# Pacing the first forty transfers of a fused attention and MoE kernel by the fourth ahead

## The chip, the cores and the metric

The kernel runs on one core of a Trainium2 chip. The metric is the time of one execution in microseconds of device time; three runs were made of the kernel before. Engines are called as in the profile: PE is TensorE's matmul, PEld its weight load, DVE VectorE, ACT ScalarE, POOL GpSimd, SP SyncE. SP computes nothing here; it issues transfers (DMAs).

## The reference, cut to what matters

Chunked attention comes first: 4 batches of 8 heads, sequences of 768, head size 64. Each chunk of 32 queries looks at 16 keys to its left, its own 32, 8 to its right and 8 memory keys, 64 in all. The attention's output, as a matrix x of 3072 tokens by 512, then goes through a two-layer block with a rational function between the layers.

```python
for c in range(nc):
    k_full = np.concatenate([mem_k, k_ctx], axis=2)
    v_full = np.concatenate([mem_v, v_ctx], axis=2)
    scores = scale * np.matmul(q_c, k_full.transpose(0, 1, 3, 2))
    a = np.exp(scores - np.max(scores, axis=-1, keepdims=True))
    a = a / (np.sum(a, axis=-1, keepdims=True) + 1e-09)
    out[:, :, c_start:c_end] = np.matmul(a, v_full)
...
h = x @ w_in
P = a[0] + a[1] * h + a[2] * h2 + a[3] * h3
Q = 1.0 + np.abs(b[0]) * np.abs(h) + np.abs(b[1]) * h2
return ((P / (Q + 1e-06)) @ w_out).astype(np.float32)
```

The weights w_in (512 x 2048) and w_out (2048 x 512) are handed over as 64-bit floats, bit for bit.

## The kernel before, in words

**Tiling.** The 3072 tokens are six blocks of 512. The hidden size 2048 is sixteen slices of 128. A step n stands for one (block, slice): g1 (L480) makes h, 128 x 512, in 12 matmuls (L489); the chain of lines L557 to L614 computes the rational function on ACT, DVE and POOL; g2 (L491) adds its product with w_out into four accumulators in another 12 matmuls (L504). Each weight and each x is split into a high and a low part, hence three matmuls for every product.

**Attention.** A unit is (block i, pair of heads p). For the first two blocks its pieces are: the load of queries and keys (q), of values (v); scores on PE (b, L361), maximum, difference and exponential on DVE and ACT (L369, L379, L396), zeroing of absent keys on POOL (L392), transposes on PE (c, L412), a copy (L419), the product with the values (d, L428) and the sums (L434), the division (L444), transposes back (L454), and the split into x_hi and x_lo.

**Weights.** Each weight tile arrives as raw 64-bit words (w, w_load) and is converted by five tokens: A (ACT, L183), B (DVE, L187), C (DVE, L192), H (ACT, L199), L (POOL, L204).

**Order.** The first part of the program is a list of tokens written out by hand (SEQ); function hand turns each into instructions, which every engine keeps in program order. All transfers go through one helper, load (L145), and nearly all of them through SP's queue, in program order. The transfers are counted in this document from 1 in the order in which load is called:

- 1: w_in slice 0. 2 and 3: queries and keys of unit (0,0), one transfer for each head. 4 and 5: (0,2). 6 and 7: (0,1). 8 and 9: values of (0,0). 10 and 11: queries and keys of (0,3). 12: w_out slice 0. 13: the six parameters, a few bytes.
- 14 and 15: values of (0,2). 16 and 17: values of (0,1). 18: w_in slice 1. 19 and 20: queries and keys of (1,0). 21 and 22: values of (0,3). 23 and 24: w_in slices 3 and 2.
- 25 to 28: queries and keys of (1,1) and (1,2). 29 and 30: values of (1,0). 31: w_in slice 4. 32: w_out slice 1. 33 and 34: values of (1,1). 35: w_in slice 5. 36 and 37: values of (1,2). 38: w_out slice 2. 39 and 40: queries and keys of (1,3).

Queries and keys are 64 rows of 4,608 bytes (294,912 bytes), values 64 rows of 4,096 (262,144), a weight half 128 rows of 4,096 (524,288).

The framework tells the landing of a transfer by a semaphore and uses eight of them in turn, so that SP holds a transfer back until the eighth ahead of it has landed. A transfer also waits until its buffer is clear: for the memset of its pads or for the last reader of the buffer's former content.

Of the kernel before, what the change touches and what calls it, by code (L numbers as in the profile page):

```python
# [37 lines left out]
XL_POOL = [(0, 0), (0, 2), (1, 0), (1, 1), (1, 2)]  # L38
WARM = 14
CLEAR = [("qk", 0, "vp"), ("qk", 3, "ap"), ("qk", 1, "pv"), ("qk", 2, "vv"), ("v", 1, "pa"), ("v", 2, "pv"), ("v", 0, "pp"), ("v", 3, "pp")]  # L40
LEAD = 22
WHEN = dict(b=0, m=1, x=2, c=2, z=3)
WAIT = 4
# [46 lines left out]
def attn_moe(ctx, tc, qk, vm, w, ab, out, seq):  # L90
# [50 lines left out]
    def pin(ins):  # L141
        if pinned[0]:
            tc.keep_in_program_order(ins)

    def load(dst, src, queue=nc.sync):  # L145
        ins = queue.dma_start(out=dst, in_=src)
        if in_order[0]:
            tc.keep_in_program_order(ins)

# [12 lines left out]
    def w_load(kind, j):  # L162
        if kind == "in":
            raws[j] = slot(RAW_SLOTS[j], "w_raw", U32)
        if j < WHOLE:
            load(half(raws[j], kind), half(w_bits_of[j][:, :4 * DM], kind))
        elif kind == "in":
            load(raws[j], w_bits_of[j][:, :4 * DM])
# [55 lines left out]
    def load_qk(i, p, t, queue=nc.sync):  # L224
        u = unit.setdefault((i, p), {})
        u["q"], u["k"] = [], []
        for h in range(2):
            load(rows(t[:, h * NK:h * NK + NK + NQ], h), qk[i, p, h], queue)
        for c in range(NC):
            u["q"].append(t[:, NK + c * CHUNK:NK + (c + 1) * CHUNK])  # L230
            first = t[:, start_in(c):start_in(c) + KEYS]
            u["k"].append(bass.AP(first.tensor, first.offset, [list(first.ap[0]), [NK + NQ, 2], [1, KEYS]]))
# [392 lines left out]
    def plan(n, kind, i, p):  # L625
        att.setdefault((n, kind), []).append((i, p))

    units = [(i, p, base) for i in range(3, NBLK)
             for p, base in enumerate(BASES.get(i, [first[i] - LEAD + 4 * p for p in range(NPAIR)]))]
    went = []  # L630
# [34 lines left out]
    def begin():  # L665
        pick = {"a": nc.scalar, "v": nc.vector, "p": nc.gpsimd}
        for name, n, who in CLEAR:
            engines = [pick[x] for x in who]
# [175 lines left out]
```

## Time and profile before

| what | value |
|---|---|
| median of 3 runs | 599.34 us (598.25 to 599.51) |
| the profiled execution's own time | 598.73 us |
| its span, first to last instruction | 596.9 us |
| around the span | 1.8 us |
| granted TensorE clock, mean of the span | 1.000 |
| PE busy | 586.8 us, 98% |
| DVE, ACT, POOL busy | 464.9, 401.9, 406.4 us |

The span is what the profile explains; the 1.8 us around it are the start and the end of the program. The profiled execution was 0.61 us shorter than the median. A PE that is busy for 98% of the span leaves about 10 us in which it had nothing to do. Slices in the page are a fortieth of the span, 14.9 us.

### The profile page before, as it was taken

To read this page: it belongs to the slowest core of one execution; us is meant where nothing else is said; L and a number is where in the kernel's file an instruction comes from. 1 tells how busy PE (TensorE), PEld (TensorE's weight loads), DVE (VectorE), ACT (ScalarE), POOL (GpSimd) and SP (SyncE) were. 2 spreads that over 40 slices of the span, in tenths; PEclk is the share of its full clock that TensorE was granted. 3 is DMA by queue.
4 is the path that set the end of the run, shared out by engine and by line. 5 is a ranking of instruction groups with operands and counts; after the bars stand their busy time and mean duration, and the time that the engine had idled before them with its cause. 6 is when DMAs were issued, how large, how long until landed. Compare 5 with 4: busy or idle time off the path is not lost.

```text
span 596.9 us, 13088 instructions
## 1 busy us (share of the span) xinstructions
PE 586.8 (98%) x5111; PEld 478.4 (80%) x5111; DVE 464.9 (78%) x762; ACT 401.9 (67%) x665; POOL 406.4 (68%) x376
## 2 busy tenths in 40 slices
PE   7899999999999999999999999999999999999997
PEld 6677888888787878878888888888888888888886
DVE  5899999898797759888877778787787766666673
ACT  4699999898667655656566666565765656755673
POOL 5468998798546766576677576766667677667682
PEclk9999999999999999999999999999999999999999
DMA  8965346230345344332331422312510100100001
GB/s 304 406 206 213 146 177 212 72 128 13 124 131 165 98 151 127 94 111 72 99 87 50 154 43 87 94 36 81 178 36 1 37 10 9 71 1 1 0 1 70
DMA packets 34591, 61.14 MB, mean 102 GB/s; under 512 B 4066, under 2 KB 20706, under 8 KB 34146
## 3 DMA queue, kind: packets, MB, share of 16 engines
q1 hardware_dynamic: 34386, 60.18, 30.6%
q8 instruction: 40, 0.66, 0.5%
q14 instruction: 21, 0.17, 0.1%
q10 hardware_dynamic: 144, 0.13, 0.1%
HBM read 44.56 MB, written 7.34 MB: 87 GB/s over the span
## 4 chain that ended last, share of the span: by engine, by line
PE 95%; DVE 2%; ACT 1%; DMA 1%; issue 0%; SPq 0%; POOL 0%; DVEq 0%
PE h L489 44%; PE o L504 43%; PE pairs L315 2%; PE pairs L293 2%; PE pa L428 1%; PE pa L361 1%; DMA qk<-in_qk_dram 1%; PE pa L412 1%; PE pa L454 0%; DVE e L379 0%; PE pa L434 0%; ACT e L396 0%; DVE ct L602 0%; ACT eT L419 0%; PE warm L663 0%
## 5 line engine op out<-in xcount | busy, mean ns | idle before, releaser
L489 PE MATMUL h<-x_hi,w_hl 128*128 128x512 f32 x768 | 240.3, 394 | 0.4 <-DVE ct L602 0.3
L504 PE MATMUL o<-w_hl,ghi 128*128 128x512 f32 x768 | 236.8, 390 | 0.0
L566 POOL TENSOR_TENSOR cy<-cy,ha 128x512 f32<-128x512 f32 x96 | 124.6, 1298 | 140.4 <-ACT cy L562 135.8
L504 PEld LDWEIGHTS o<-w_hl,ghi 128*128 128x128 f32 x768 | 143.9, 188 | 29.8 <-ACT v_main L546 0.2
L489 PEld LDWEIGHTS h<-x_hi,w_hl 128*128 128x128 f32 x768 | 141.7, 188 | 32.4 <-DVE ct L602 1.1
L489 PE MATMUL h<-x_lo,w_hl 128*128 128x512 f32 x384 | 150.0, 391 | 0.2 <-POOL x_lo L467 0.2
L504 PE MATMUL o<-w_hl,glo 128*128 128x512 f32 x384 | 150.0, 391 | 0.0
L614 POOL TENSOR_TENSOR glo<-ct,ghi 128x512 fp32r<-128x512 f32 x95 | 122.9, 1294 | 9.1 <-ACT ghi L609 3.2
L594 DVE SCALAR_TENSOR_TENSOR ct<-ct,par,h 128x512 f32<-128x512 f32 x82 | 61.2, 746 | 56.2 <-ACT h L590 55.5
L575 DVE TENSOR_TENSOR ct<-ct,h 128x512 f32<-128x512 f32 x96 | 65.6, 684 | 39.4 <-ACT ct L571 37.8
L586 ACT ACTIVATE h<-cy 128x512 f32<-128x512 f32 x82 | 49.1, 599 | 69.5 <-DVE ct L579 56.1
L557 ACT ACTIVATE ha<-h 128x512 f32<-128x512 f32 x96 | 57.4, 598 | 54.4 <-PE h L489 54.3
L607 POOL TENSOR_TENSOR ghi<-ct,zero 128x512 fp32r<-128x512 f32 x81 | 84.2, 1040 | 2.5 <-PE o L504 1.2
L504 PEld LDWEIGHTS o<-w_hl,glo 128*128 128x128 f32 x384 | 72.1, 188 | 16.8 <-POOL glo L614 1.6
L489 PEld LDWEIGHTS h<-x_lo,w_hl 128*128 128x128 f32 x384 | 72.1, 188 | 16.1 <-POOL x_lo L467 0.6
L562 ACT ACTIVATE cy<-ha,bab 128x512 f32<-128x512 f32 x96 | 78.4, 817 | 2.6
L571 ACT ACTIVATE ct<-h,par 128x512 f32<-128x512 f32 x96 | 73.6, 766 | 5.6 <-PE h L489 5.5
L579 DVE SCALAR_TENSOR_TENSOR ct<-ct,par,h 128x512 f32<-128x512 f32 x96 | 71.6, 746 | 3.0
L602 DVE SCALAR_TENSOR_TENSOR ct<-h,ct 128x512 f32<-128x512 f32 x82 | 56.5, 689 | 2.6
L598 DVE SCALAR_TENSOR_TENSOR h<-cy,h 128x512 f32<-128x512 f32 x82 | 56.5, 689 | 0.0
L590 ACT ACTIVATE h<-h 128x512 f32<-128x512 f32 x82 | 47.7, 582 | 2.6
L204 POOL TENSOR_TENSOR w_hl<-w_raw,w_hl 128x512 fp32r<-128x512 f32 x32 | 42.0, 1318 | 6.4 <-ACT w_hl L199 5.7
(80 smaller groups left out, 461.9 us busy)
## 6 DMA issues: line engine op xcount, KB each, us to landing
w_raw<-in_w_dram SPq DMA_DIRECT2D x26, 512.0 KB, 5.9
qk_pairs<-in_qk_dram SPq DMA_DIRECT2D x16, 576.0 KB, 4.2
v_main<-in_vm_dram SPq DMA_DIRECT2D x16, 512.0 KB, 5.1
out_dram<-v_main SPq DMA_DIRECT2D x23, 256.0 KB, 2.3
qk<-in_qk_dram SPq DMA_DIRECT2D x16, 288.0 KB, 5.8
eT<-blocks SPq DMA_DIRECT2D x64, 64.0 KB, 2.1
xf<-blocks SPq DMA_DIRECT2D x64, 64.0 KB, 2.1
v_main<-in_vm_dram SPq DMA_DIRECT2D x12, 256.0 KB, 6.4
```

The source lines that it names most:

```text
L489: pin(nc.tensor.matmul(h, lhsT=wt[:, cols], rhs=xt[i][:, ct, :], start=ct == m == 0, stop=ct == NCT - 1 and m == 2))
L504: ins = nc.tensor.matmul(o, lhsT=gt[:, cols], rhs=wt, start=begin and m == 0, stop=end and m == 2)
L557: pin(nc.scalar.activation(c["ha"], c["h"], AF.Abs))
L562: pin(nc.scalar.activation(c["y"], c["ha"], AF.Identity, scale=B1, bias=B0))
L566: pin(nc.gpsimd.tensor_tensor(c["y"], c["y"], c.pop("ha"), op=ALU.mult))
L571: pin(nc.scalar.activation(c["t"], c["h"], AF.Identity, scale=A3, bias=A2))
L575: pin(nc.vector.tensor_tensor(t, t, h, op=ALU.mult))
L579: pin(nc.vector.scalar_tensor_tensor(t, t, A1, h, op0=ALU.add, op1=ALU.mult))
L594: pin(nc.vector.scalar_tensor_tensor(t, t, A0, r, op0=ALU.add, op1=ALU.mult))
L598: pin(nc.vector.scalar_tensor_tensor(r, yy, QC, r, op0=ALU.add, op1=ALU.mult))
L607: pin(nc.gpsimd.tensor_tensor(ghi, chain[z]["t"], zero.broadcast_to([P, TB]), op=ALU.add))
L614: pin(engine.tensor_tensor(glo, chain.pop(z)["t"], gh[z].bitcast(F32), op=ALU.subtract))
```

## The change

A list of the transfers made so far is kept. Of the first forty, each from the fifth on gets a dependency on the one made four before it, of the kind that is kept with a semaphore: SP may issue it only when that transfer has landed. Sizes, order, queue, buffers and all other instructions are as before.

```diff
+AHEAD = 4
+PACED = 40
...
+    sent = []
+
     def load(dst, src, queue=nc.sync):
         ins = queue.dma_start(out=dst, in_=src)
+        sent.append(ins)
+        if AHEAD < len(sent) <= PACED:
+            tc.add_manual_dep(ins.ins, sent[-1 - AHEAD].ins.name, mybir.DependencyInfo(mybir.DependencyClass.Sync, mybir.DependencyReason.DATA), reason="pace")
         if in_order[0]:
             tc.keep_in_program_order(ins)
```

## Rows read from the trace of the kernel before

**Rows 1.** The page: the DMA's share and rate in 40 slices.

```profile
DMA  8965346230345344332331422312510100100001
GB/s 304 406 206 213 146 177 212 72 128 13 124 131 165 98 151 127 94 111 72 99 87 50 154 43 87 94 36 81 178 36 1 37 10 9 71 1 1 0 1 70
```

**Rows 2.** The page: the chain that ended last, shares of the span by engine.

```profile
PE 95%; DVE 2%; ACT 1%; DMA 1%; issue 0%; SPq 0%; POOL 0%; DVEq 0%
```

**Rows 3.** The chain that ended last in order of time, first 60 us: start, us, what.

```profile
2.19 4.35 DMA qk<-in_qk_dram
...
6.68 1.97 PE pa L361 x32
...
16.34 1.13 issue
17.47 0.60 PE pa L412 x4
...
28.30 2.69 PE h L489 x10
...
49.25 2.91 PE h L489 x12
```

**Rows 4.** Busy time of each engine in four stretches; the last three columns are PEclk, DMA share, GB/s.

```profile
5.00:13.00 8.00, 5.66 (x104) 4.87 (x104) 3.35 (x6) 1.79 (x3) 3.71 (x6) 1.00 0.98 355
13.00:30.00 17.00, 15.42 (x306) 11.98 (x305) 14.63 (x30) 11.13 (x22) 6.88 (x10) 1.00 1.03 404
39.00:43.00 4.00, 3.76 (x83) 3.00 (x85) 4.00 (x8) 3.47 (x7) 2.73 (x5) 1.00 0.89 274
80.00:83.00 3.00, 3.00 (x15) 2.47 (x14) 2.93 (x5) 3.00 (x6) 3.00 (x4) 1.00 1.02 416
```

**Rows 5.** SP's issues in order of time: start us, us, what; between 7 and 39 us.

```profile
7.41 1.18 SPq L146 DMA_DIRECT2D qk<-in_qk_dram  x2
...
12.37 0.36 SPq L146 DMA_DIRECT2D w_raw<-in_w_dram  x1
...
32.06 0.33 SPq L146 DMA_DIRECT2D w_raw<-in_w_dram  x1
36.26 1.11 SPq L146 DMA_DIRECT2D v_main<-in_vm_dram  x2
37.42 0.58 SPq L146 DMA_DIRECT2D w_raw<-in_w_dram  x1
38.04 1.11 SPq L146 DMA_DIRECT2D qk<-in_qk_dram  x2
```

**Rows 6.** Issue to landing of single transfers, us: numbers 4, 10, 18, 35, 36, 39.

```profile
qk<-in_qk_dram SPq DMA_DIRECT2D x1, 288.0 KB, 4.4
...
qk<-in_qk_dram SPq DMA_DIRECT2D x1, 288.0 KB, 4.9
...
w_raw<-in_w_dram SPq DMA_DIRECT2D x1, 512.0 KB, 7.1
...
w_raw<-in_w_dram SPq DMA_DIRECT2D x1, 512.0 KB, 3.9
...
v_main<-in_vm_dram SPq DMA_DIRECT2D x1, 256.0 KB, 2.9
...
qk<-in_qk_dram SPq DMA_DIRECT2D x1, 288.0 KB, 5.8
```

**Rows 7.** PE in order of time, 6 to 36 us: start, us, what, idle before.

```profile
10.98 0.66 PE L412 MATMUL pa<-ident,e 128*128 128x128 f32 x4 [0.66 <-POOL e L392]
...
14.50 1.08 PE L361 MATMUL pa<-qk 128*32 128x128 f32 x32
...
32.51 1.08 PE L361 MATMUL pa<-qk 128*32 128x128 f32 x32
```

**Rows 8.** ACT in order of time: the readers of transfers 18, 23, 31, and one wait.

```profile
20.13 0.68 ACT L183 ACTIVATE stage<-w_raw 128x512 f32<-128x512 f32 x1
21.89 0.59 ACT L458 CAST x_hi<-pa 128x512 fp32r<-128x512 f32 x1 [1.08 <-PE pa L454]
...
26.09 0.64 ACT L183 ACTIVATE stage<-w_raw 128x512 f32<-128x512 f32 x1
...
35.79 0.67 ACT L183 ACTIVATE stage<-w_raw 128x512 f32<-128x512 f32 x1
```

**Rows 9.** The page: the queue that fetches instructions (packets, MB, share).

```profile
q8 instruction: 40, 0.66, 0.5%
```

## The prediction, made before the result was known

> **What bounds the kernel now.** I read the chain that ended last first: 95% of it is PE, 1% DMA [rows 2]. A transfer can only matter where PE is not yet fed. In order of time [rows 3] the chain opens with the first queries and keys (2.19 to 6.54 us), hops between PE and the other engines, and from 28.3 us on shows matmuls of lines 489 and 504. What to see: the forty paced transfers lie in this opening; behind it the work on PE is fixed, so an opening that ends x us later moves the end by about x.
>
> The second view is the DMA's rate. The page's first two slices move 304 and 406 GB/s, most later ones under 210 [rows 1]. By stretch the rate is 355 GB/s from 5 to 13 us and 404 from 13 to 30, at a share of 0.98 and 1.03 [rows 4]. A full DMA is the case in which holding transfers back can be free: what would have queued behind other transfers queues at SP instead.
>
> The third view is SP. The old limit is visible: transfer 10, issued at 7.41 us, lands 4.9 us later, at 12.3; transfer 18, eight behind, goes out at 12.37 [rows 5, 6]. So SP paces already, by eight, and the change halves that depth.
>
> **The change, part by part.** It removes no transfer and no byte and moves no step on another engine. It adds 36 waits (transfers 5 to 40). What each wait itself costs SP is taken as nothing: SP computes nothing, and the landing that it waits for is microseconds away. Behind a waiting transfer stand only SP's later transfers; ACT, DVE, POOL and PE wait for their data and for nothing else of SP.
>
> *When the issues come.* Transfer 10 must now wait for 6, and so on; in the full stretch a transfer took 4.4 to 7.1 us from issue to landing [rows 6] because up to seven others were ahead of it. With three ahead, the issue comes some 2 to 4 us later (my estimate: the queue is shorter by four transfers, each 0.65 us for 262 KB and 1.3 us for 524 KB at 404 GB/s, 2.6 to 5.2 us in all).
>
> *Whether the data come later.* This is the one cost that the trace does not show: the rate at a depth of four. Upper bound: 404 GB/s, nothing lost. By the lone transfers: transfer 36, 262 KB of values with nothing ahead of it, lands 2.9 us after its issue, transfer 35, a weight half of 524 KB, 3.9 us after [rows 6]. Four in flight, each issued as the fourth ahead lands, give 4 x 262 KB in 2.9 us, 361 GB/s, for the small ones; for weights 4 x 524 KB in 3.9 us is 538, above the 404 that the DMA carries, so nothing is lost there. That three weight transfers alone filled it (416 GB/s from 80 to 83 us [rows 4]) agrees. Lower bound: 274 GB/s from 39 to 43 us [rows 4], where SP had four to six transfers out in a burst that began at 36.26 us [rows 5].
>
> I take the middle value, from the lone transfers, as it is measured at the sizes in question and includes the start of an idle DMA, which a depth of four largely avoids. Transfers 5 to 34 are 11 of queries and keys (0.295 MB), 12 of values (0.262 MB) and 6 weight halves (0.524 MB): 6.39 MB small, 3.15 MB weights, 9.54 MB. At 361 and 404 GB/s they take 17.7 + 7.8 = 25.5 us. Transfer 4 lands at 2.92 + 4.4 = 7.3 us, so transfer 34 would land near 32.8 us, where the DMA now falls idle a little after 30.
>
> *What slack the readers have.* With the rate r from 7.3 us on, the readers' times give the r below which each is late:
> - Transfer 5 belongs to the scores computed right behind the first ones. They are not what PE waits for next: PE idles 0.66 us before 10.98 us, for POOL [rows 7]. Transfer 5 itself waits only for transfer 1, while 2 to 4 still stream, so it isn't late.
> - Transfer 11 (2.00 MB behind transfer 4), read at 14.50 us [rows 7]: 2.00 / 7.2 = 278 GB/s.
> - Transfer 18 (4.10 MB), read by ACT at 20.13 [rows 8]: 4.10 / 12.8 = 320 GB/s. ACT then idles 1.08 us before 21.89 for PE [rows 8], so being a microsecond late costs nothing; that puts the real bound at 4.10 / 13.9 = 295.
> - Transfer 23 (5.73 MB), read at 26.09: 305 GB/s. Transfer 28 (7.44 MB), read at 32.51 [rows 7]: 295. Transfer 31 (8.49 MB), read at 35.79 [rows 8]: 298.
>
> At 361 to 404 GB/s nobody is late. **The sum:** waits 0, issues 0 (hidden behind the data still in the DMA), landings up to a microsecond later, hidden by slack of 1.4 to 5 us: 0 us on the path.
>
> *The tail of the pace.* From transfer 35 on compute sets the issue (32.06, 36.26 us [rows 5]) and the fourth ahead has long landed. Only transfer 40 meets its wait: number 36 lands at 36.26 + 2.9 = 39.2 us, so number 40 goes out near 39.2 instead of 38.6, and 41 behind it. Both stand behind 37, 38 and 39 (39 lands at 38.04 + 5.8 = 43.8 us [rows 6]); cover over 4 us, cost 0. Nothing behind transfer 40 is paced.
>
> One rule speaks against this. The Trainium skill's "DMA: Bandwidth & Descriptors", section "Latency and other measured facts", gives an HBM access 0.2 us on average and 2 us at high load, as the main part of a transfer's fixed cost. As an estimate from that page, a small transfer under load would take 2.9 + 1.8 = 4.7 us, four of them 223 GB/s, and the sum would be transfer 34 at 50 us and an end some 10 us later, about 609 us. The trace has no depth of four under load; its worst stretch shows 274.
>
> **Against the runs.** The profiled execution took 598.73 us, span 596.9 and 1.8 around it. With 0 added it stays so; the median of the runs stands 0.61 us higher, and I forecast that: 599.3 us.
>
> **The rivals.**
>
> *Slower: depth four leaves the DMA short.* One mechanism: each landing comes too late to keep the next transfer's data running, and the rate from 7.3 us on falls to the 274 of the slow burst. It decides below about 300 GB/s. Then transfer 18 lands at 7.3 + 4.10/0.274 = 22.3 us, 2.1 late (1.1 behind ACT's idle time), number 23 2.1 late, number 31 at 38.3, 2.5 late. The opening ends up to 2.5 us later: 601.8 us. For it: the small transfers' own rate already stood at 355 GB/s from 5 to 13 us, before the depth of eight held anything back, and the slow burst had four to six. Against: that burst began from an idle DMA, and three weights filled it. To cost over 1.2 us the rate must be under some 285.
> In that family, the loaded latency itself is a case: transfer 39 took 5.8 us with three ahead of it [rows 6]; if every small one took 4.7 us at a depth of four the end would be near 609. I give it 2 in 100, since the three ahead of number 39 explain most of its time. The page above is its source.
>
> *Faster: less in flight serves the urgent ones sooner.* The first queries and keys are on the path (4.35 us [rows 3]). Transfer 1 lands at about 4.3 us; two more of 0.295 MB at 404 GB/s would land at 5.7, not 6.54: at most 0.8 us. And PE stands for 1.2 us before 17.47 us for nothing that the profile shows ("issue", 1.13 us of the chain [rows 3]); its instructions are fetched by DMA too (40 packets of 16 KB [rows 9]), and a shorter queue could shorten that. Both whole: 599.3 - 0.8 - 1.1 = 597.4 us. Against: transfers 2 and 3 leave before any paced one, and what is ahead of them does not change; of the stall most would be taken by the next wait, for DVE. The Trainium skill's same page, section "Queues, rings and completion order", says that each DMA engine goes round its queues packet by packet, by which a fetch wouldn't stand behind the whole backlog and this rival would keep only the 0.8; no row here shows that.
>
> *The wait is not there:* the framework could take the order on one queue as enough. SP's issues would stand where they are now: 599.3 us too.
>
> **How the numbers follow.** A measurement of this kernel can tell about 0.2%, 1.2 us, from no change. Landings hidden: 0.69, and the wait not there 0.04, both 599.3 us and within 0.2%; of the slow rival's mild form (rates of 285 to 300, under 1.2 us) 0.02 is in the same class: same 0.75. Slower by more: 0.17 for rates down to 274 (up to 601.8) and 0.02 for the loaded latency: 0.19. Faster by more needs both parts of the fast rival: 0.06. The range goes from 598.2, the fast rival's first part and the runs' own spread, to 602.0, the lower bound of the rate; it leaves out the full fast rival and the loaded latency.
>
> **What would show each step.** Right: SP's issues of transfers 6 to 34 later by 2 to 4 us and each shortly behind the landing of the fourth ahead; issue to landing down to about 3 us; 13 to 30 us still at 360 GB/s or more; ACT's reads of weights near 20.1, 26.1 and 35.8 us and the first full g1 steps where they were. Wrong: under 300 GB/s from 7 to 30 us with ACT or PE waiting for a transfer of weights or of queries and keys; or a first score matmul before 6.0 us, or no stall before 17.47 us and an end over 1.2 us earlier.

## The result, and the profile after

The changed kernel takes 602.97 us (median of 5 runs, 601.88 to 604.48) against 599.34: a ratio of 1.0061, 95% interval 1.0046 to 1.0077, so slower by 0.5 to 0.8%. I had forecast no change, 599.3, with a range up to 602.0. The profiled execution took 604.48 us, its span 602.6.

The page, slice by slice, where [rows 1] stood before:

```profile
DMA  7885735303244444433212512312510100100001
GB/s 244 267 286 175 290 119 191 130 22 134 80 133 146 125 110 139 150 86 96 95 39 89 164 36 79 107 35 77 174 33 10 36 5 14 71 1 1 0 1 70
```

The first two slices carry 244 and 267 GB/s in place of 304 and 406, and the third more than before: the same bytes, spread over a longer time. By stretch, to be held against the first two lines of [rows 4], and the stretch of a slow clock:

```profile
5.00:13.00 8.00, 5.24 (x99) 4.65 (x102) 3.28 (x5) 1.76 (x3) 3.72 (x6) 1.00 0.86 282
13.00:30.00 17.00, 12.85 (x254) 10.47 (x249) 9.83 (x21) 7.22 (x16) 2.83 (x5) 0.84 0.81 265
...
24.50:31.30 6.80, 6.80 (x60) 5.58 (x61) 3.43 (x8) 3.97 (x9) 0.20 (x1) 0.50 0.94 306
```

From 13 to 30 us the DMA moves 265 GB/s at a share of 0.81, where it moved 404 at 1.03, and PE is busy for 12.85 us of the 17 instead of 15.42. Who waits for the data is in PE's timeline (start, us, what, idle before and what ended it):

```profile
16.33 1.08 PE L368 MATMUL pa<-qk 128*32 128x128 f32 x32 [1.40 <-DMA qk<-in_qk_dram]
...
23.45 1.08 PE L435 MATMUL pa<-v_main,eT 128*32 128x128 f32 x32 [2.07 <-DMA v_main<-in_vm_dram]
```

All lines below 147 of the old file are 7 further down: L368 is L361, L435 is L428, L496 is L489, L190 is L183. The scores of unit (0,3), at 14.50 before [rows 7], now wait for transfer 11, and the values of unit (0,1) for transfer 17. The chain that ended last, in order of time, shows how transfer 17 came to be late:

```profile
7.72 4.39 DMA v_main<-in_vm_dram
12.11 0.02 issue
12.12 5.18 DMA w_raw<-in_w_dram
17.30 0.02 issue
17.32 0.56 ACT stage L190
17.89 5.32 DMA v_main<-in_vm_dram
23.20 0.25 issue
23.45 1.08 PE pa L435 x32
...
33.70 3.28 PE h L496 x12
...
55.27 2.91 PE h L496 x12
```

And SP's row for transfers 16 and 17:

```profile
17.32 1.11 SPq L150 DMA_DIRECT2D v_main<-in_vm_dram  x2
```

Transfer 8 lands at 12.11 and releases 12; 12 lands at 17.30 and releases 16; SP issues 17 right behind 16, at 17.89; 17 lands at 23.20. The step on ACT, which the view puts between, is not what 17 waited for: ACT reads the weights of transfer 12 there, until 18 us, and does not touch the buffer of 17. Two of those steps are landings that something waited for, and in both the wait was over 5 us. The piece at 55.27 us answers to the one at 49.25 in [rows 3]: 6.0 us late. The span's end is 5.7 us late.

**The clock.** From 24.5 to 31.3 us TensorE ran at half clock, 1.2 instead of 2.4 GHz; just before, PE had idled 2.07 us and run one group of matmuls (23.45 to 24.5 us) at full clock. Two rows of before and one of after show what that stretch added:

```profile
20.18 1.08 PE L428 MATMUL pa<-v_main,eT 128*32 128x128 f32 x32
...
25.09 1.08 PE L428 MATMUL pa<-v_first,eT 128*32 128x128 f32 x32 [0.15 <-ACT eT L419]
```

```profile
30.99 1.23 PE L435 MATMUL pa<-v_first,eT 128*32 128x128 f32 x32
```

The values of unit (0,1) start 3.3 us late (23.45 against 20.18), those of unit (0,3), which wait for no transfer here, 5.9 us late (30.99 against 25.09): some 2.6 us more in this execution. It is not the loss itself: of the 13 runs of this kernel, the five here and the eight of the next section, the seven with a mean granted clock of 0.999 or 1.000 have a mean of 602.4 us, the six at 0.993 to 0.997 one of 602.9.

### The profile page after: what moved, and what is told of

Read it like the earlier page. It is cut to its first block, busy times and chain, and to the rows that moved or that the text cites. A ratio compares the mean times of both kernels' runs of the same rounds, so it can differ in the third digit from the quotient of the medians.

```text
span 602.6 us, 13090 instructions
## 1 busy us (share of the span) xinstructions
PE 589.6 (98%) x5111; PEld 481.0 (80%) x5111; DVE 465.0 (77%) x762; ACT 402.3 (67%) x665; POOL 406.4 (67%) x376
## 4 chain that ended last, share of the span: by engine, by line
PE 94%; DMA 2%; POOL 1%; DVE 1%; ACT 1%; issue 0%; POOLq 0%
PE h L496 44%; PE o L511 43%; PE pairs L322 2%; PE pairs L300 2%; DMA v_main<-in_vm_dram 2%; PE pa L435 1%; DMA w_raw<-in_w_dram 1%; PE pa L368 1%; PE pa L461 1%; POOL v_main L229 0%; PE pa L419 0%; POOL v_first L229 0%; POOL qk L229 0%; DVE ct L609 0%; PE pa L441 0%
## 5 line engine op out<-in xcount | busy, mean ns | idle before, releaser
L496 PE MATMUL h<-x_hi,w_hl 128*128 128x512 f32 x768 | 241.0, 395 | 0.4 <-DVE ct L609 0.3
L496 PEld LDWEIGHTS h<-x_hi,w_hl 128*128 128x128 f32 x768 | 141.9, 188 | 32.5 <-DVE ct L609 1.1
L496 PE MATMUL h<-x_lo,w_hl 128*128 128x512 f32 x384 | 150.1, 391 | 0.0
L496 PEld LDWEIGHTS h<-x_lo,w_hl 128*128 128x128 f32 x384 | 72.2, 188 | 15.9 <-DVE x_lo L477 0.4
```

What stands on the lines that cost most here:

```text
L496: pin(nc.tensor.matmul(h, lhsT=wt[:, cols], rhs=xt[i][:, ct, :], start=ct == m == 0, stop=ct == NCT - 1 and m == 2))
```

## The experiments

Twelve kernels were run, each beside the kernel before on the same chip. The ratios are to that kernel's runs there (medians of 598.8 to 599.0 us).

**The change once more.** No edit.

> The changed kernel once more, for a second profile and more runs with the granted clock of each. Theory A (PE waits for late transfers): 602 to 604 us again, 260 to 300 GB/s from 7 to 30 us, PE idle on transfers, though not needfully on the same ones. Theory D (a good part of the loss is the half clock that the first profile shows from 24.5 to 31.4 us): runs with a granted clock of 1.0 are 1.5 us or more faster than those with a stretch at half clock.

Measured: 602.53 us (600.88 to 603.24, 8 runs), 1.0048 [1.0032, 1.0065]. Its profile has a clock of 1.000 throughout the opening, a span of 601.1 us, and other late transfers. PE's timeline and the chain in order of time:

```profile
26.34 1.35 PE L368 MATMUL pa<-qk 128*32 128x128 f32 x32 [0.83 <-DMA qk<-in_qk_dram]
...
29.41 1.08 PE L435 MATMUL pa<-v_first,eT 128*32 128x128 f32 x32 [1.72 <-DMA v_first<-in_vm_dram]
```

```profile
7.65 4.09 DMA v_main<-in_vm_dram
...
11.75 5.91 DMA w_raw<-in_w_dram
...
18.84 5.99 DMA w_raw<-in_w_dram
24.82 0.02 issue
24.84 0.02 SPq L150
24.85 0.03 issue
24.88 4.39 DMA v_first<-in_vm_dram
29.27 0.14 issue
29.41 1.08 PE pa L435 x32
...
53.54 2.91 PE h L496 x12
```

This is the pace itself, in the chain: 18 lands at 24.82 us and only then does SP issue 22, whose reader stood ready. The values of unit (0,3) start at 29.41 instead of 25.09 us, 4.3 late; the piece at 53.54 is 4.3 late; the span is 4.2 longer. So the opening's delay goes to the end one for one, and half a clock is not needed for it. Theory A holds. D does not: the runs at a clock of 0.999 or 1.000 are 0.5 us faster than the others, not 1.5. The half clock can account for the 1.5 us by which the first profile's execution lies above the median, and not for the median.

**The depth.** `AHEAD` alone is changed: 8, 6, 2 and 1.

```diff
-AHEAD = 4
+AHEAD = 8
```

> Each of transfers 9 to 40 waits for the eighth ahead instead of the fourth: the depth that the framework's eight semaphores already keep. Theory A (the depth of four is the cause, the waits as such cost nothing): 599.3 us, DMA 400 GB/s or more from 13 to 30 us, first full g1 step at about 37.4 us. Theory B (waits or their instructions on SP cost something of their own): later than 599.3 by a good part of the 3.6 us, and transfers issued later than their eighth-ahead landing.

> Depth six. Theory A1 (the rate grows with the depth until the DMA is full): between depth four's 277 GB/s and the full 404, about 340 GB/s from 7 to 42 us; the needs of the readers are under 320 GB/s, so the time is back within 1 us of 599.3. Theory A2 (only a depth of eight keeps the DMA engines from running dry): under 300 GB/s and about 602 us.

> Depth two. Theory A with the latency of lone transfers (2.9 us for values, about 3 for queries and keys, 3.9 for weights): two in 3.2 us on average, 0.318 MB each, about 200 GB/s, transfer 34 at about 55 us and an end near 614 us. Theory A with the latency seen at depth four (4.8 us): about 130 GB/s, transfer 34 near 80 us, 635 us or more.

> Depth one: each transfer alone, so issue to landing is its lone latency in the opening itself. If the lone latency of the two transfers that I read (2.9 and 3.9 us) holds for all: medians of 2.9 to 3.0 us for the small and 3.6 to 3.9 for weights, about 100 GB/s, transfer 34 near 100 us, end near 660 us. If the opening's transfers are slow of themselves: medians over 4 us, 70 GB/s, end over 680 us.

Depth 8: 599.26 us, 1.0008 [0.9997, 1.0018]; depth 6: 598.81 us, 0.9998 [0.9989, 1.0008]; depth 2: 623.12 us, depth 1: 681.45 us (one run each). The stretch from 13 to 30 us at depths 8 and 6 and from 10 to 60 us at 2 and 1 (PEclk, DMA share and GB/s are last):

```profile
13.00:30.00 17.00, 16.07 (x307) 12.56 (x308) 14.96 (x30) 11.25 (x23) 6.89 (x10) 1.00 1.02 407
```

```profile
13.00:30.00 17.00, 15.45 (x311) 11.80 (x304) 14.08 (x29) 10.63 (x21) 6.86 (x10) 1.00 0.94 324
```

```profile
10.00:60.00 50.00, 36.42 (x532) 29.28 (x533) 28.48 (x53) 23.43 (x42) 13.62 (x21) 0.78 0.62 187
```

```profile
10.00:60.00 50.00, 24.12 (x328) 19.73 (x328) 13.30 (x26) 8.69 (x18) 2.92 (x6) 0.67 0.32 94
```

And issue to landing of the paced transfers, the median per kind, at depth 1, then 4 (the first profile of the change), then in the kernel before:

```profile
w_raw<-in_w_dram SPq DMA_DIRECT2D x7, 512.0 KB, 3.5
qk<-in_qk_dram SPq DMA_DIRECT2D x10, 288.0 KB, 3.1
v_main<-in_vm_dram SPq DMA_DIRECT2D x8, 256.0 KB, 2.8
```

```profile
w_raw<-in_w_dram SPq DMA_DIRECT2D x6, 512.0 KB, 5.2
qk<-in_qk_dram SPq DMA_DIRECT2D x11, 288.0 KB, 4.8
v_main<-in_vm_dram SPq DMA_DIRECT2D x8, 256.0 KB, 4.4
```

```profile
qk<-in_qk_dram SPq DMA_DIRECT2D x11, 288.0 KB, 6.5
w_raw<-in_w_dram SPq DMA_DIRECT2D x6, 512.0 KB, 6.6
v_main<-in_vm_dram SPq DMA_DIRECT2D x8, 256.0 KB, 6.4
```

The rate grows with the depth all the way: 94, 187, 265, 324, 407 GB/s at 1, 2, 4, 6 and 8 (the first two over a longer stretch). The second transfer in flight adds 93 GB/s; from there each further one adds 30 to 42, as each takes longer. The mean transfer has 9.54 MB / 30 = 0.318 MB; four of them in about 4.7 us are 271 GB/s, eight in 6.5 us 391: rate and latency agree with each other at each depth. The waits as such cost nothing (depth 8), and depth 6, at 324 GB/s, is just above the 320 that the most pressed reader needed. Theory A came true at depth 8 and A1 at depth 6 (312 GB/s from 7 to 42 us, where it had about 340). Depth 2 fell between its two theories (614 and 635). At depth 1 the latencies and the rate are those of the first theory, with the lone latencies (about 100 GB/s and 660 us), and yet the end is the second one's, over 680. Neither had counted a slow clock (0.67 of full from 10 to 60 us, 0.937 over the span); that it makes up the difference is not shown.

**Parts of the pace.** Only the first 18 are paced, or only those from the 19th on:

```diff
-PACED = 40
+PACED = 18
```

```diff
-        if AHEAD < len(sent) <= PACED:
+        if 18 < len(sent) <= PACED:
```

> Only transfers 5 to 18 are paced by four. Theory A (what stalls PE are the waits for transfers 11 and 17, read at 14.5 and 20.2 us before): the whole loss stays, about 603 us, though the DMA catches up behind transfer 18 (over 380 GB/s from 25 to 33 us). Theory C (the loss is spread over all forty): about half of it, 601 us.

> Only transfers 19 to 40 are paced by four. Theory A: their readers have slack of 2.7 us and more, and fall late by less than that as the first 18 come as before: 599.3 to 600 us. Theory C (spread over all): about 601 us, with ACT waiting for weights at 26 and 36 us.

First 18: 600.86 us, 1.0033 [1.0021, 1.0045]. From 19 on: 599.10 us, 1.0002 [0.9991, 1.0013]. The late part alone costs nothing though it runs at 297 GB/s from 13 to 30 us: its readers have the slack that I had worked out. The early part alone costs 2 of the 3.5 us; theory A had said all, and C's 601 us came. In the second kernel it is the other way round: A's 599.3 to 600 us holds within the noise, and C's 601 does not. So neither theory covers both: the parts cost 2.0 and 0.1 us alone and 3.5 together. The DMA did catch up behind transfer 18 in the first kernel (412 GB/s from 25 to 33 us): SP issues 22 by 21 us in place of 24.88, and the values of unit (0,3) start at 26.93, 1.8 us late instead of 4.3. With both parts paced nothing catches up.

**Transfers 14 to 22 freed.**

```diff
-        if AHEAD < len(sent) <= PACED:
+        if AHEAD < len(sent) <= PACED and not 14 <= len(sent) <= 22:
```

> The pace of four without transfers 14 to 22, whose readers were the ones that PE waited for (11 and 17 in one profile, 20 and 22 in the other). Theory A (the loss is PE waiting for those few): most of it gone, 599.3 to 600.3 us, transfer 22 landed by 25 us. Theory C (the loss is spread over all forty, each late landing costs): 601 us or more.

599.36 us, 1.0001 [0.9989, 1.0013]. The other 27 waits cost nothing. From 13 to 30 us the rate is 313 GB/s, and PE waits 0.7 us for one pair of values and 2.5 us in all for queries and keys, 2.0 of which are the first two, as before:

```profile
13.00:30.00 17.00, 15.00 (x303) 11.80 (x296) 14.32 (x30) 11.11 (x22) 6.90 (x10) 1.00 0.90 313
```

```profile
PE pa L368 <- DMA qk<-in_qk_dram: 2.5, 2, 2.0
...
PE pa L435 <- DMA v_first<-in_vm_dram: 0.7, 1, 0.7
```

Theory A holds. So without the hold on these nine, which stand between the DMA's start and PE's full load, there is no loss; what they would cost if they alone were held was not run.

**The tiny transfer.** Number 13, a few bytes, no longer counts as one of the four:

```diff
-        sent.append(ins)
-        if AHEAD < len(sent) <= PACED:
+        if src is not ab:
+            sent.append(ins)
+        if src is not ab and AHEAD < len(sent) <= PACED - 1:
```

> Transfer 13, the parameters' few bytes, is left out of the count and of the pace; the 39 others wait for the fourth ahead among themselves. Theory A: one more large transfer is in flight from 14 to 17, which moves transfer 17 a microsecond or so forward: 601.5 to 602.5 us, between depth four and depth six. Theory E (the tiny transfer that takes one of four places is the main cause): below 600.5 us.

601.12 us, 1.0032 [1.0017, 1.0046]: about 1.4 us better than the change by the medians on the same chip (1.2 by the means, with a standard error of 0.4 worked out from the 9 and 8 runs), though the two intervals against the kernel before overlap (the change there: 1.0032 to 1.0065). From 13 to 30 us the rate is 303 GB/s. That is under theory A's 601.5 to 602.5 and over theory E's 600.5. A pace by count lets a few bytes fill a place meant for 300 KB; that is part of the loss and not the main one.

**Twice as many halves.** The kernel before, without a pace, each of its first forty transfers (of 64 rows or more) made as two:

```diff
-        ins = queue.dma_start(out=dst, in_=src)
...
+        n = dst.shape[0] // 2
+        whole = made[0] > 40 or n < 32
+        for a, s in ((dst, src),) if whole else ((dst[:n], src[:n]), (dst[n:], src[n:])):
+            ins = queue.dma_start(out=a, in_=s)
```

> The kernel before (no pace), with each of the first forty transfers of 64 or 128 rows made as two of half the rows: the framework's depth of eight now holds the bytes of four whole transfers. Theory F (the bytes in flight set the rate): as at depth four, 260 to 290 GB/s from 7 to 30 us, and 601.5 to 603 us. Theory G (the number of transfers in flight sets it, each keeping its place whatever its size): over 370 GB/s and 599 to 600 us. SP issues twice as many in the opening, 0.4 to 0.6 us each, which is about 0.5 x 60 = 30 us of SP's time and may bound the rate near 310 GB/s by itself.

611.63 us, 1.0205 [1.0189, 1.0222], 229 GB/s from 7 to 30 us; neither theory's numbers came. It tells nothing between F and G: SP issues one every 0.6 us with hardly a pause, which for halves of 0.131 to 0.262 MB is about the rate that was seen.

```profile
2.03 7.59 SPq L152 DMA_DIRECT2D qk<-in_qk_dram  x12
9.71 2.45 SPq L152 DMA_DIRECT2D v_main<-in_vm_dram  x4
```

Twelve issues in 7.59 us are 0.63 us each. SP need not be the only bound: from 30 to 42 us the DMA's share was 0.98 at 242 GB/s, so each byte kept the engines busy 1.6 times as long as in the kernel before (1.03 at 404). Whether bytes or transfers in flight set the rate stays open.

**Trying to win.** The chain starts with the first queries and keys, and the opening goes to the end one for one. In the kernel before, the first weight half was put behind the first two transfers, and in a second kernel behind the first four (the head of SEQ's first line):

```diff
-w q00 b00 m00 q02 A q01
+q00 w b00 m00 q02 A q01
```

```diff
-w q00 b00 m00 q02 A q01
+q00 b00 m00 q02 w A q01
```

> The kernel before (no pace), with the first two transfers of queries and keys ahead of the first weight half instead of behind it. Theory A (the opening starts with these two, and what it gains or loses goes to the end one for one): they land near 5.2 us instead of 6.54, the first scores start 1 to 1.3 us earlier, and the end comes 0.5 to 1.3 us earlier, 597.9 to 598.5 us; the weight half lands near 6 us, ahead of its need at 10 us. Theory H (the opening is held by another chain, POOL's clearing of buffers or the conversion of weights): scores earlier, the end the same, 599 us.

> The kernel before (no pace), with the first weight half behind the first four transfers of queries and keys instead of ahead of them (putting it behind the first two made the next two late, read at 8.1 us). Theory A (an opening that ends earlier moves the end as much): first two landed near 5.2 us, next two near 7, the weight half near 8.5, before its reader's product is needed at 10.7; scores 1 to 1.4 us earlier and the end 0.5 to 1.2 us earlier, 597.8 to 598.5 us. Theory H (other waits of the opening take the place, POOL's clearing or the conversion that now starts at 8.5): 598.8 to 599.5 us, no change, or later where the conversion's delay is carried on.

Both lost: 600.90 us, 1.0032 [1.0021, 1.0043], and 601.47 us, 1.0031 [1.0012, 1.0050]. PE's timeline of the first, the scores of the first two units:

```profile
5.70 1.08 PE L361 MATMUL pa<-qk 128*32 128x128 f32 x32 [1.01 <-DMA qk<-in_qk_dram]
10.31 1.93 PE L361 MATMUL pa<-qk 128*32 128x128 f32 x32 [3.52 <-DMA qk<-in_qk_dram]
```

The first scores come 1 us earlier, the second nearly 2 us later. No more bytes stand ahead of transfer 5 than before; they start later. In the kernel before, the weight half streams while SP still waits for the buffers of the queries to be cleared; behind the queries it is issued only at 2.84 us, and from 1 to 3 us the DMA moves 0 and 28 GB/s instead of 41 and 217. In the second kernel it is ACT, whose program has the weight's first conversion ahead of the first exponential:

```profile
10.81 0.64 ACT L183 ACTIVATE stage<-w_raw 128x512 f32<-128x512 f32 x1 [7.10 <-DMA w_raw<-in_w_dram]
11.38 0.62 ACT L396 ACTIVATE e<-e 128x512 f32<-128x512 f32 x1
```

ACT stands for 7.10 us until the weight lands at 10.8, and the exponential that was at 10.12 before follows at 11.38. No version here beats the kernel before.

## Why the prediction was wrong

*The step that failed* is the price of the one thing that the trace of before did not show, the rate at a depth of four. I took "the middle value, from the lone transfers", 361 GB/s for the small ones and the DMA's 404 for weights, 374 in all. Measured: 265 and 254 GB/s from 13 to 30 us in the two profiles of the change. The lone latency was right (2.8, 3.1 and 3.5 us at depth 1), but it doesn't hold with three others in flight: at depth 4 the medians are 4.1 to 5.6 us over both profiles (only the four transfers into v_first had 3.3 in one of them). The rows of before had held a sign of it: transfer 4, issued with 1, 2 and 3 in flight, took 4.4 us [rows 6], and four of 0.295 MB in 4.4 us are 268 GB/s. The row that seemed to agree, three weights at 416 GB/s [rows 4], is a burst and no steady pace: they were issued within a microsecond, at 77.70 to 78.55 us, and a fourth, of 1 MB, followed at 81.50. The lower bound that I had from the burst at 39 us, 274 [rows 4], was the nearer row: mixed transfers, four to six in flight. I set it aside because it began from an idle DMA; at a depth of four the DMA has idle time again and again. Its share tells so: 0.81 / 1.03 leaves 21% of the engines' time unused, and the 0.81 moved 265 GB/s where a full share moved 404, so each byte took 0.81/265 over 1.03/404, 1.20 times as long. The two together make 404 into 265.

*The slow rival was the right mechanism*, and its 601.8 us came within 1.2 of the median. It was sized on too few readers: transfers 17 and 22, which made the loss in the two profiles, were not on my list. By the same working, 22 has 5.21 MB behind transfer 4 and is read at 25.09 us, so it needs 293 GB/s; in the second profile it landed at 29.27, 21.7 us behind transfer 4, at 240. Transfer 18, which was on the list at 2.1 us late, was 4.4 and 4.7 late: ACT idled for it 3.75 and 4.03 us and read it at 24.49 and 24.84 us instead of 20.13. The working also assumed one rate throughout, while a paced chain makes late ones later: 12 waits for 8, 22 for 18, each a landing of 4 to 6 us.

*What the Trainium skill had to say.* The estimate from "DMA: Bandwidth & Descriptors", section "Latency and other measured facts", 4.7 us for a small transfer under load, is close to the 4.1 to 4.8 measured at depth four; there the trace agrees in the number, and no run shows whether HBM's load is the reason. The 223 GB/s and 609 us worked out from it did not come, as weights bring twice the bytes in 5.2 to 5.6 us. I had given this case 2 in 100 and explained the long latencies by queueing alone.

*The other steps.* The waits cost nothing (depth 8: 1.0008). SP held the transfers to the landing of the fourth ahead, as the chain shows. That the issues would come 2 to 4 us later was too little for the late ones: transfer 10 left 3.0 us later (10.40 against 7.41), 18 left 6.1 and 6.5 us later (18.47 and 18.84 against 12.37). The tail of the pace and the slack of the late readers were right (from 19 on: 1.0002). The fast rival found nothing: the first queries and keys landed no sooner but took 4.6 to 4.8 us instead of 4.3 to 4.4, so that PE's first scores start at 7.10 and 6.97 us against 6.68. And in the profile at depth 8 PE's 1.2 us stall before 17.47 us was absent, a wait of 0.69 us for POOL stood in its place, and the time was the same, 599.26 us. That the opening goes to the end one for one was right (4.3 us at 29 us, 4.3 at 53, 4.2 at the end).

## What to carry to other kernels

A DMA that is full at a depth of eight says nothing of its state at four: read the rate of a stretch where about that many transfers were in flight, and take it even when a lone transfer's latency promises more. To find what a slower DMA costs, list the need of every reader (bytes ahead of it by its time) and not a sample; here the needs worked out lay at 278 to 320 GB/s; 324 cost nothing and 265 cost 3.5 us. The rate of a whole stretch is only a guide: 297 GB/s from 13 to 30 us cost nothing where the first 18 had come unpaced, and 303 cost 2 us where they had not. Where a wait must be added, put it behind the point where the bound engine is fully fed.

## What the runs showed of the hardware that I had not expected

The rate of transfers of some 0.3 MB rose with each step of depth up to eight (94, 187, 265, 324 and 407 GB/s), with no level reached at four. PE's idle gap of 2.07 us before 23.45 us was followed by 6.8 us at half clock in one profile of the change. In these rows the length of the gap does not tell when that happens: the gaps of 2.40 and 2.28 us before the first scores of the change's two profiles were not followed by it, and in the kernel paced from 19 on a gap of 2.04 us before the first scores was, with 1.1 us of matmuls and another gap of 0.83 us between, from 8.8 to 12.3 us; that kernel's time was still the time of before (1.0002). And one kernel's late transfers differ from run to run (11 and 17 in one profile, 20 and 22 in the other): the changed kernel's runs spread over 3.6 us, 600.88 to 604.48.
